# Attention and two feed-forward layers on one core: one more row group in seven products, a shared last query tile, wider idle matmuls

## The chip, the cores and the metric

The kernel runs on one core of a Trainium2 chip. The metric is the device time in microseconds (us) of one execution, inputs in device memory at its start and the output there at its end. TensorE (PE in the profile) multiplies; VectorE (DVE), ScalarE (ACT) and GpSimd (POOL) do the elementwise work; SyncE (SP) issues nearly all DMAs, in order.

## The reference, cut to what matters

```python
# attention: 4 batches, 8 heads, 576 positions, head size 64, 128 random features
def phi(x):
    h = einsum('bhsd,md->bhsm', x, omega) - sum(x * x) / 2
    return exp(h - max(h, -1)) / sqrt(128)
q_p, k_p = phi(q * scale), phi(k * scale)
kv, z = einsum('bhsm,bhsd->bhmd', k_p, v), sum(k_p, 2)
x = einsum('bhsm,bhmd->bhsd', q_p, kv) / (einsum('bhsm,bhm->bhs', q_p, z)[..., None] + 1e-6)
x = x.transpose(0, 2, 1, 3).reshape(2304, 512)
h = x @ moe_w_in;  x = (h - tanh(h)) @ moe_w_out              # layer 1, d_ff = 2048
h = x @ moe2_w_in; out = (h * sigmoid(1.702 * h)) @ moe2_w_out  # layer 2, d_ff = 2048
```

## The kernel before, in words

The program is one stream per engine, in the order in which the code issues it; there is no scheduler. It has three stages.

**Attention** (`period(k)`, k = 0 to 15, and two tails) takes two heads at a time: 16 pairs. The pairs are software-pipelined: in one period TensorE projects the queries of pair k (`att_a`, L133) and the keys of pair k+1 (`att_b`, L161, L164), transposes the normalised result of pair k-2 (`att_e`, L237), builds key times value of pair k (`att_c`, L188, L192) and the numerators with their denominators of pair k-1 (`att_d`, L210). A pair's 576 queries are four tiles of 128 and a fifth that holds the last 64. In `att_d` each tile and head is one fp32 matmul: the exponentials of 128 queries are the stationary operand, key times value with its extra column (65 columns) the moving one. So there are 10 a pair, in two PSUM tiles (tags y2 and y3): six for tiles 0 to 2, four for tiles 3 and 4. The fifth tile starts at query 448, so it computes 64 queries a second time (`s0 = min(st * 128, S - 128)`), and only `tq[:, 64:128]` of its transpose is used. Every fp32 matmul but a transpose shows as two records.

Then VectorE adds the epsilon, takes the reciprocal and multiplies (`att_d_norm`, L222 to L224), TensorE transposes into y2 and y3, ScalarE rounds the transposed tile to the upper part (`att_e_hi`, L251) and VectorE subtracts it to get the lower part (`att_e_lo`, L256). Both parts are stored to the DRAM tensor `xs`, one DMA each (two each in the first batch, whose first 512 positions stay in SBUF). `xh` and `xl` have one buffer, so the next pair's write waits for the store. L210 of the next pair writes y2 and y3 again, so it waits for L256. VectorE also subtracts the maximum (L147) that GpSimd reduced over partitions (L143), and with ScalarE unpacks layer 1's weights (L293 to L327) in two periods of three.

**Layer 1** makes x in blocks of 512 rows and is not touched.

**Layer 2** has three row blocks of 768, each seen as two halves of 384, and eight pairs of 256 hidden columns: 24 groups (`GROUPS`), the last eight (n = 16 to 23) on the third block, with pair 7 first (`LAST`). Each group's hidden part h is made by a seven-product scheme (`h_prod`, L868): P1 to P7, six matmuls each, one a slot; a group has seven slots (`SLOTS`), and `q = 7 * n + s` counts them. The group's y part is made one group later. There are two ways: `y_chunk` (L889), eight chunks of six matmuls in `hs` banks; or, for the groups with `yform(n)`, that is `YG <= n < YE` (17 to 22), seven products P1 to P7 of six matmuls (`y_prod`, L929) in two PSUM tiles `ya` and `yc` of two banks each, with operands formed on GpSimd (`forms`) and combined output weights `wos`. `y_chunk` at a block's first group copies into `yacc`, later ones add (L899); `y_add` (L938) always adds.

The input forms of the third block (`xprep_ticks(2, ...)`) are 14 ticks, popped one a slot from q = 101: each casts on ScalarE (L432) and subtracts on GpSimd (kt = 0) or VectorE (kt = 1, L433), and some make a difference on VectorE first (L582). Their loads are issued at group 14, slot 0. The combined output weights of a pair are three more ticks (`L2_STICKS`): sums on GpSimd (L440), then two splits (L432, L433), each stored to `wfs`; in the code before, pair 7 has none.

At the program's start two matmuls on zeros (`warm_up(pt("y0")[:, :320], 2)`, L601) run while the first inputs arrive.

Of the kernel before, what the change touches and what calls it, by code (L numbers as in the profile page):

```python
# [25 lines left out]
DV = D + 1  # L26
# [29 lines left out]
L2_TICKS = {(0, 1): "a", (0, 5): "b", (1, 1): "s", (1, 2): "c", (1, 3): "h", (1, 5): "d", (1, 6): "o", (2, 0): "e"}  # L56
L2_STICKS = {2: "f", 3: "g", 6: "i"}
SLOTS = ("P1", "P7", "P6", "P4", "P5", "P2", "P3")
XID = dict(P2=0, P1=1, P7=2, P6=3, P4=4, P5=5, P3=6)

YG, YE = 2 * NPAIR + 1, 3 * NPAIR - 1
YP = ("P3", "P1", "P2", "P6", "P7", "P5", "P4")
# [4 lines left out]
def body(ctx, tc, qT, kT, v, om, w1, w2, out):  # L67
# [58 lines left out]
    def att_a(i):  # L126
# [7 lines left out]
        return a  # L134

    def att_a_copy(i, tiles, j):
        if j == 0:
            pqs[i] = ap.tile([128, 2, S], F32, tag="pq", name="pq", bufs=2)
        pq, r = pqs[i], rest[i]
        nc.scalar.copy(out=pq[:, j, 0:512], in_=tiles[j])  # L140
        nc.scalar.copy(out=pq[:, j, 512:S], in_=r[j][:, :S - 512])  # L141
        mqs[i, j] = ap.tile([128, S], F32, tag="mq", name="mq", bufs=2)
        nc.gpsimd.partition_all_reduce(  # L143
            mqs[i, j], pq[:, j, :], channels=128, reduce_op=bass.bass_isa.ReduceOp.max)

    def att_sub(i, j):
        nc.vector.tensor_tensor(out=pqs[i][:, j, :], in0=pqs[i][:, j, :], in1=mqs.pop((i, j)), op=ALU.subtract)  # L147

    def att_exp(i, j):
        nc.scalar.activation(out=pqs[i][:, j, :], in_=pqs[i][:, j, :], func=AF.Exp)  # L150

# [49 lines left out]
    def att_d(i):  # L201
        pq, kvz = pqs.pop(i), kvzs.pop(i)
        tags = ("y0", "y1") if i == N16 - 1 else ("y2", "y3")
        for g, d, tag in (((0, 1, 2), pn1, tags[0]), ((3, 4), pn2, tags[1])):
            pn = pt(tag)
            for k, st in enumerate(g):
                s0 = min(st * 128, S - 128)
                for j in range(2):
                    c = (2 * k + j) * DV
                    nc.tensor.matmul(  # L210
                        pn[:, c:c + DV], pq[:, j, s0:s0 + 128], kvz[:, j * DV:j * DV + DV],
                        start=True, stop=True)
            d[i] = pn
        xts[i] = ap.tile([128, ST, 2, D], F32, tag="xt", name="xt", bufs=2)
# [25 lines left out]
    def att_e_parts(i, tiles):  # L240
        tp, tq = tiles
        b, p = divmod(i, NP)
        xh = ap.tile([128, S], F32R, tag="xh", name="xh", bufs=1)
        xl = ap.tile([128, S], F32R, tag="xl", name="xl", bufs=1)
        xd = xblk[0, 0]
        h0, l0 = (xd[:, 0, p, :], xd[:, 1, p, :]) if b == 0 else (xh[:, :512], xl[:, :512])
        return (h0, l0, tp), (xh[:, 512:], xl[:, 512:], tq[:, 64:128]), xh, xl

    def att_e_hi(parts):
        for h, l, src in parts[:2]:  # L250
            nc.scalar.copy(out=h, in_=src)  # L251

    def att_e_lo(i, parts):
        b, p = divmod(i, NP)
        for h, l, src in parts[:2]:
            nc.vector.tensor_tensor(out=l, in0=src, in1=h.bitcast(F32), op=ALU.subtract)  # L256
        c0 = 512 if b == 0 else 0
        for hl, t in ((0, parts[2]), (1, parts[3])):
            nc.sync.dma_start(out=xs[hl, p, :, b * S + c0:b * S + S], in_=t[:, c0:].bitcast(F32))
            if b == 0:  # L260
                nc.sync.dma_start(out=xs[hl, p, :, :512], in_=parts[0][hl].bitcast(F32))

# [202 lines left out]
    def conv_ticks(p, pairs, place=None):  # L465
# [208 lines left out]

    warm_up(pt("y0")[:, :320], 2)
    tiles, mx = att_b(0)
# [395 lines left out]
    for n in range(NG + 1):  # L1072
        sb, j = GROUPS[min(n, NG - 1)]
        for s in range(7):
# [50 lines left out]
            if xticks:  # L1125
                if 3 <= q < 98 and q != 6 or q > 100:
                    xticks.popleft()()
# [6 lines left out]
            if ticks and at >= 0:  # L1134
                for x in L2_TICKS.get((at // 7 % 2, s), "") + (L2_TICKS.get((2, s), "") if at >= 14 and at // 7 % 2 == 0 else ""):
                    if ticks[0][0] == x:
                        ticks.popleft()[1]()
            if sticks and at >= 14 and at // 7 % 2 == 0 and s in L2_STICKS:
                assert sticks[0][0] == L2_STICKS[s]
                sticks.popleft()[1]()  # L1140
            if n == 14 and s == 0:
                assert not ticks and not sticks
# [62 lines left out]
```

## Time and profile before

| | |
|---|---|
| time, median of 3 runs | 893.46 us (893.02 to 893.53) |
| the profiled execution | 894.37 us, its span 892.6 us |
| TensorE busy | 887.0 us, 99% of the span, 5154 matmul records |
| VectorE, ScalarE, GpSimd busy | 624.1, 575.5 and 528.3 us |
| HBM traffic | 171 GB/s over the span |

The span runs from the first to the last instruction; the 1.8 us beside it are what lies around it. A busy time is the union of an engine's records, and a record is longer than the step from one start to the next, since each is pipelined into the one before: lengths of steps are read from starts.

### The profile page before, as it was taken

What the parts mean: (1) busy time and instruction counts of PE and PEld (TensorE: products, weight loads), DVE (VectorE), ACT (ScalarE), POOL (GpSimd) and SP (SyncE); (2) the same over time, 40 slices, a digit from 0 to 9 for tenths busy, and PEclk for the clock granted to TensorE, in tenths of its full rate; (3) what the DMA queues carried; (4) which work ended last, traced back from release to release, by engine and by line L of the source; (5) the groups of instructions that cost most, each with busy time, mean ns of one, the idle gap of its engine ahead of it and who ended that gap; (6) DMA issues with size and microseconds to landing.
All of it is one profiled execution on the core that took longest, in us unless ns stands there. A gap on an engine that the chain in (4) does not pass through costs nothing.

```text
span 892.6 us, 14447 instructions
## 1 busy us (share of the span) xinstructions
PE 887.0 (99%) x5154; PEld 812.3 (91%) x5154; DVE 624.1 (70%) x956; ACT 575.5 (64%) x1205; POOL 528.3 (59%) x424
## 2 busy tenths in 40 slices
PE   9999999999999999999999999999999999999998
PEld 7999988888899888888898899999999999999997
DVE  5999978766666665787767457477877778445555
ACT  6999978787777766877667644446565554434442
POOL 3555535566656655777765556537657565347774
PEclk9999999999999999999999999999999999999999
DMA  7888855043353440695471560824553241376751
GB/s 237 249 265 258 280 172 176 24 142 104 109 189 117 143 142 24 186 325 197 166 270 48 207 217 3 289 97 179 201 203 145 90 131 48 112 301 235 296 224 71
DMA packets 55815, 153.38 MB, mean 172 GB/s; under 512 B 6336, under 2 KB 13120, under 8 KB 52672
## 3 DMA queue, kind: packets, MB, share of 16 engines
q1 hardware_dynamic: 55600, 152.15, 49.3%
q8 instruction: 40, 0.66, 0.3%
q10 hardware_dynamic: 144, 0.33, 0.1%
q14 instruction: 31, 0.25, 0.1%
HBM read 105.27 MB, written 47.19 MB: 171 GB/s over the span
## 4 chain that ended last, share of the span: by engine, by line
PE 97%; DVE 2%; POOL 1%; DMA 0%; issue 0%; ACT 0%; POOLq 0%
PE y L391 22%; PE hs L353 22%; PE y L868 19%; PE hs L889 17%; PE yb L929 5%; PE y L210 4%; PE y L192 2%; PE y L133 2%; PE hs L161 1%; PE hs L868 1%; PE y L237 1%; PE hs L164 1%; POOL mq L143 1%; DVE pq L147 0%; DMA kt<-kT 0%
## 5 line engine op out<-in xcount | busy, mean ns | idle before, releaser
L353 PE MATMUL hs<-xb,w 128*128 128x512 f32 (+1 forms) x960 | 209.2, 368 | 0.0
L353 PEld LDWEIGHTS hs<-xb,w 128*128 128x128 f32 x960 | 167.5, 189 | 30.0
L868 PE MATMUL y<-x,win 128*128 128x384 f32 x966 | 193.1, 334 | 0.0
L391 PE MATMUL y<-ghi,w 128*128 128x512 f32 (+1 forms) x640 | 192.4, 368 | 0.1
L367 POOL TENSOR_TENSOR glo<-wq,ghi 128x512 fp32r<-128x512 f32 x72 | 101.0, 1403 | 136.9 <-ACT ghi L365 135.3
L868 PEld LDWEIGHTS y<-x,win 128*128 128x128 f32 x966 | 169.7, 188 | 0.0
L889 PE MATMUL hs<-g,wout 128*128 128x384 f32 x864 | 169.1, 334 | 0.0
L383 DVE COPY_PREDICATED wq<-m,t 128x512 f32<-128x512 uint16 x72 | 88.6, 1230 | 104.8 <-POOL wq L381 103.7
L889 PEld LDWEIGHTS hs<-g,wout 128*128 128x128 f32 x864 | 151.4, 188 | 0.4 <-DVE yacc L938 0.3
L391 PEld LDWEIGHTS y<-ghi,w 128*128 128x128 f32 x640 | 116.6, 189 | 20.6 <-issue 0.5
L977 POOL TENSOR_TENSOR g<-sg,g 128x384 fp32r<-128x384 f32 x84 | 96.7, 1159 | 48.0 <-ACT g L976 24.9
L391 PE MATMUL y<-glo,w 128*128 128x512 f32 (+1 forms) x320 | 117.8, 368 | 0.0
L899 DVE TENSOR_TENSOR yacc<-hs,yacc 128x384 f32<-128x384 f32 x120 | 65.7, 552 | 51.4 <-PE hs L889 50.9
L381 POOL TENSOR_TENSOR wq<-wq,s 128x512 f32<-128x512 f32 x70 | 90.6, 1294 | 18.6 <-DVE wq L380 18.6
L143 POOL PARTITION_ALL_REDUCE mq<-pq x32 | 67.0, 2140 | 53.1 <-ACT pq L141 45.0
L373 ACT ACTIVATE s<-hs 128x512 f32<-128x512 f32 x72 | 43.0, 598 | 61.4 <-PE hs L353 61.3
L391 PEld LDWEIGHTS y<-glo,w 128*128 128x128 f32 x320 | 60.4, 189 | 9.9
L964 ACT ACTIVATE sg<-y 128x384 f32<-128x384 f32 x57 | 28.1, 494 | 62.9 <-DVE y L949 58.1
L304 DVE SCALAR_TENSOR_TENSOR raw<-raw 128x512 int32<-128x512 int32 x57 | 62.8, 1101 | 1.6
L938 DVE TENSOR_TENSOR yacc<-yb,yacc 128x768 f32<-128x768 f32 x42 | 40.2, 958 | 33.7 <-PE yb L929 33.5
L365 ACT CAST ghi<-wq 128x512 fp32r<-128x512 f32 x72 | 44.3, 616 | 27.8 <-DVE wq L383 27.7
L380 DVE SCALAR_TENSOR_TENSOR wq<-wq,hs 128x512 f32<-128x512 f32 x72 | 49.1, 681 | 13.3 <-ACT t L375 13.2
(146 smaller groups left out, 1470.5 us busy)
## 6 DMA issues: line engine op xcount, KB each, us to landing
raw<-w SPq DMA_DIRECT2D x57, 512.0 KB, 4.6
xb<-xs SPq DMA_DIRECT2D x24, 512.0 KB, 6.0
win<-wfi SPq DMA_DIRECT2D x9, 1280.0 KB, 6.7
wout<-wfo SPq DMA_DIRECT2D x9, 1024.0 KB, 7.4
wos<-wfs SPq DMA_DIRECT2D x6, 1024.0 KB, 8.8
vt<-v SPq DMA_DIRECT2D x16, 325.0 KB, 3.9
kt<-kT SPq DMA_DIRECT2D x15, 320.0 KB, 3.4
qt<-qT SPq DMA_DIRECT2D x16, 288.0 KB, 3.2
```

Source lines behind the costliest of these rows:

```text
L143: nc.gpsimd.partition_all_reduce(mqs[i, j], pq[:, j, :], channels=128, reduce_op=bass.bass_isa.ReduceOp.max)
L304: nc.vector.scalar_tensor_tensor(out=c, in0=c, scalar=3, in1=z, op0=ALU.logical_shift_left, op1=ALU.bitwise_or)
L353: nc.tensor.matmul(h[:, j * n:j * n + n], w[:, 0, a, kt * 128:kt * 128 + 128], x[:, c, kt, :n], start=(k == 0), stop=(k == 11))
L367: nc.gpsimd.tensor_tensor(out=lo, in0=g, in1=hi.bitcast(F32), op=ALU.subtract)
L380: nc.vector.scalar_tensor_tensor(out=w, in0=w, scalar=QC, in1=h, op0=ALU.add, op1=ALU.mult)
L381: (nc.vector if si < 2 else nc.gpsimd).tensor_tensor(out=w, in0=w, in1=s, op=ALU.mult)
L383: nc.vector.copy_predicated(out=w, mask=m.bitcast(mybir.dt.uint16), data=t)
L391: nc.tensor.matmul(y[d][:, :n], w[:, 1, a, d * 128:d * 128 + 128], g[c][:, j * n:j * n + n], start=(first and j == 0 and k == 0), stop=(la ...
L868: nc.tensor.matmul(dst, w[:, WID[name], a, kt * 128:kt * 128 + 128], xt[:, kt, c, :], start=(first and k == 0), stop=(k == 5), skip_group_ ...
L889: nc.tensor.matmul(dst, wout[j][:, f, a, d * 128:d * 128 + 128], gt[n, f, t][:, c, :], start=(k == 0), stop=(k == 5))
L899: nc.vector.tensor_tensor(out=u, in0=dst, in1=u, op=ALU.add)
L977: nc.gpsimd.tensor_tensor(out=u[:, 1, :], in0=g, in1=u[:, 0, :].bitcast(F32), op=ALU.subtract)
```

## The change

It does five things.

1. `YG` goes from 17 to 16: group 16, the third block's first, makes y from seven products. As it is the first of its block, four of its `y_add`s copy into a new `yacc` (those of P3, P1, P6 and P7, in which a quarter comes first). With n even, P1's tile gets tag `ya`; a tile of tag `yc` is opened ahead of it and not used, so that `yc` has the pool's first two banks and `ya` the other two.
2. Pair 7 gets its combined weights: `f`, `g` and `i` for all pairs, in group 14 at slots 2, 3 and 5.
3. The loads of the third block's input move from group 14, slot 0, to its slot 6, and the 14 ticks from q = 101 to 114, one a slot, to q = 107 to 114, one or two a slot (`X2_TICKS`).
4. In attention the last 64 queries of both heads stand side by side in `pq` (columns 512 to 639). One matmul takes these 128 as the stationary operand and both heads' key times value (130 columns) as the moving one; each head's answer is a block of 64 by 65 in it. It takes the place of two. The fifth tile's transpose, cast and subtraction cover 128 columns and not 64, and its stores are two a part, 64 partitions by 64 columns each.
5. The two first matmuls on zeros have 400 columns and not 320.

```diff
-YG, YE = 2 * NPAIR + 1, 3 * NPAIR - 1
+YG, YE = 2 * NPAIR, 3 * NPAIR - 1
+X2_TICKS = {2: 2, 3: 2, 4: 2, 5: 1, 6: 2, 7: 1, 8: 2, 9: 2}
...
-        nc.scalar.copy(out=pq[:, j, 0:512], in_=tiles[j])
-        nc.scalar.copy(out=pq[:, j, 512:S], in_=r[j][:, :S - 512])
+        nc.scalar.copy(out=pq[:, j * 640:j * 640 + 512], in_=tiles[j])
+        nc.scalar.copy(out=pq[:, 512 + j * 64:576 + j * 64], in_=r[j][:, :S - 512])
...
-                s0 = min(st * 128, S - 128)
+                if st == 4:
+                    nc.tensor.matmul(pn[:, 2 * k * DV:2 * (k + 1) * DV], pq[:, 512:640], kvz, start=True, stop=True)
+                    continue
...
-        return (h0, l0, tp), (xh[:, 512:], xl[:, 512:], tq[:, 64:128]), xh, xl
+        return (h0, l0, tp), (xh[:, 512:], xl[:, 512:], tq[:, :128])
...
-        for hl, t in ((0, parts[2]), (1, parts[3])):
-            nc.sync.dma_start(out=xs[hl, p, :, b * S + c0:b * S + S], in_=t[:, c0:].bitcast(F32))
-            if b == 0:
-                nc.sync.dma_start(out=xs[hl, p, :, :512], in_=parts[0][hl].bitcast(F32))
+        for hl in range(2):
+            main, last = parts[0][hl].bitcast(F32), parts[1][hl].bitcast(F32)
+            nc.sync.dma_start(out=xs[hl, p, :, b * S:b * S + 512], in_=main)
+            for j in range(2):
+                q = slice(64 * j, 64 * j + 64)
+                nc.sync.dma_start(out=xs[hl, p, q, b * S + 512:b * S + S], in_=last[q, q])
...
-        extra = [(x, f) for q in pairs if q < NPAIR - 1 for x, f in dict(
+        extra = [(x, f) for q in pairs for x, f in dict(
...
-    warm_up(pt("y0")[:, :320], 2)
+    warm_up(pt("y0")[:, :400], 2)
...
+        if n == YG and name in ("P1", "P6", "P7", "P3"):
+            u = yacc[sb, t, h] = ya_tile("yacc")
+            nc.vector.tensor_copy(out=u, in_=src)
+            return
...
+                psb.tile([128, 2, 512], F32, tag="yc", name="yb", bufs=1)
...
-                if 3 <= q < 98 and q != 6 or q > 100:
+                for _ in range((3 <= q < 98 and q != 6) + X2_TICKS.get(q - 105, 0)):
...
-            if sticks and at >= 14 and at // 7 % 2 == 0 and s in L2_STICKS:
-                assert sticks[0][0] == L2_STICKS[s]
-                sticks.popleft()[1]()
-            if n == 14 and s == 0:
+            if sticks and at >= 14 and at // 7 % 2 == 0:
+                x = L2_STICKS.get(s + (n == 14 and s > 4))
+                if x:
+                    assert sticks[0][0] == x
+                    sticks.popleft()[1]()
+            if n == 14 and s == 6:
```

TensorE in attention, one pair before, from the transpose of pair k-2 to the next pair's queries (`y` are the PSUM tiles, `pq` the exponentials, `kvz` key times value):

```order
L237 MATMUL y_450<-ident,xt 128x128
L188 MATMUL y_478<-vt,kp 128x130
L192 MATMUL y_478<-vt,kp 128x65 x8
L210 MATMUL y_496<-kvz,pq 128x65 x6
L210 MATMUL y_503<-kvz,pq 128x65 x4
L133 MATMUL y_521<-qt,omd 128x512
```

The same place in the changed program:

```order
L244 MATMUL y_450<-ident,xt 128x128
L192 MATMUL y_480<-vt,kp 128x130
L196 MATMUL y_480<-vt,kp 128x65 x8
L217 MATMUL y_498<-kvz,pq 128x65 x6
L217 MATMUL y_505<-kvz,pq 128x65 x2
L213 MATMUL y_505<-kvz,pq 128x130
L134 MATMUL y_522<-qt,omd 128x512
```

Ten numerator matmuls became nine, the last of them 130 columns wide; nothing else on TensorE moved there.

SP's queue in the same stage, one pair of a later batch before:

```order
L113 DMA qt<-qT 128x576
L118 DMA kt<-kT 128x640
L259 DMA xs<-xh 128x576
L259 DMA xs<-xl 128x576
L123 DMA vt<-v 128x650
L281 DMA raw<-w 128x1024
```

And in the changed program:

```order
L114 DMA qt<-qT 128x576
L119 DMA kt<-kT 128x640
L266 DMA xs<-xh 128x512
L269 DMA xs<-xh 64x64 x2
L266 DMA xs<-xl 128x512
L269 DMA xs<-xl 64x64 x2
L124 DMA vt<-v 128x650
L289 DMA raw<-w 128x1024
```

Two stores a pair became six, all ahead of the loads of `vt` and `raw`.

TensorE in layer 2, end of group 16's hidden part and its y part before (`g` are the activated hidden parts; the h products of group 17 stand between):

```order
L868 MATMUL y_8317<-x_7856,win 128x384 x6
L889 MATMUL hs<-g_8211,wout 128x384 x3
L889 MATMUL hs<-g_8278,wout 128x384 x3
L868 MATMUL y_8292<-x_7873,win 128x384 x6
L889 MATMUL hs<-g_8211,wout 128x384 x3
L889 MATMUL hs<-g_8278,wout 128x384 x3
L868 MATMUL y_8317<-x_7903,win 128x384 x6
L889 MATMUL hs<-g_8211,wout 128x384 x3
L889 MATMUL hs<-g_8278,wout 128x384 x3
L889 MATMUL hs<-g_8211,wout 128x384 x3
L889 MATMUL hs<-g_8278,wout 128x384 x3
```

The same place after:

```order
L876 MATMUL y_8369<-x_7887,win 128x384 x6
L937 MATMUL yb<-g_8264,wout 128x384 x6
L876 MATMUL y_8345<-x_7909,win 128x384 x6
L937 MATMUL yb<-g_8331,wout 128x384 x6
L876 MATMUL y_8369<-x_7938,win 128x384 x6
L937 MATMUL yb<-fT_8382,wos 128x384 x6
L876 MATMUL y_8345<-x_7958,win 128x384 x6
L937 MATMUL yb<-fT_8409,wos 128x384 x6
```

The slot with two chunks is gone: each slot now holds one h product and one y product.

## Rows read from the trace of the kernel before

**Rows 1.** Page, busy time of each engine
```profile
PE 887.0 (99%) x5154; PEld 812.3 (91%) x5154; DVE 624.1 (70%) x956; ACT 575.5 (64%) x1205; POOL 528.3 (59%) x424
```
**Rows 2.** Stretches of one pair, sum of three: length, engines, clock, DMA share, GB/s
```profile
41.90:49.23 7.33, 7.33 (x72) 6.67 (x71) 6.96 (x16) 6.79 (x21) 4.03 (x2) 1.00 0.94 289
...
sum 21.99, PE 21.99 PEld 20.01 DVE 20.92 ACT 20.41 POOL 12.80; mean PE 7.33 PEld 6.67 DVE 6.97 ACT 6.80 POOL 4.27
```
**Rows 3.** TensorE in order of time, one pair: start, us, instruction, records
```profile
45.24 0.39 PE L188 MATMUL y<-vt,kp 128*128 128x130 f32 x2
45.46 1.90 PE L192 MATMUL y<-vt,kp 128*128 128x65 f32 x16
47.20 2.40 PE L210 MATMUL y<-kvz,pq 128*128 128x65 f32 x20
49.52 0.69 PE L133 MATMUL y<-qt,omd 64*128 64x512 f32 x1
```
**Rows 4.** VectorE in order of time, two pairs, with idle time ahead
```profile
41.41 0.17 DVE L222 TENSOR_SCALAR rc<-y 128x6 f32<-128x6 f32 x1 [0.34 <-PE y L210]
...
45.95 0.69 DVE L256 TENSOR_TENSOR xb<-y,xb 128x512 fp32r<-128x512 f32 x1
46.56 0.21 DVE L256 TENSOR_TENSOR xl<-y,xh 128x64 fp32r<-128x64 f32 x1
...
48.74 0.16 DVE L222 TENSOR_SCALAR rc<-y 128x6 f32<-128x6 f32 x1 [0.17 <-PE y L210]
```
**Rows 5.** ScalarE in order of time, the casts of one pair
```profile
45.33 0.59 ACT L251 CAST xb<-y 128x512 fp32r<-128x512 f32 x1
45.81 0.22 ACT L251 CAST xh<-y 128x64 fp32r<-128x64 f32 x1
```
**Rows 6.** Line 259, the stores: SP's issue ns min/median/max, starts, and landing
```profile
L259 SPq DMA_DIRECT2D xs<-xl x16: 320/327/558, 25.1 to 132.9; - x16
...
DMA to landing us min/median/max: 1.7/2.8/5.1
```
**Rows 7.** DMA issues, first batch: KB each, median us to landing
```profile
xs<-xb SPq DMA_DIRECT2D x8, 256.0 KB, 2.9
...
xs<-xh SPq DMA_DIRECT2D x4, 32.0 KB, 2.2
xs<-xl SPq DMA_DIRECT2D x4, 32.0 KB, 2.7
```
**Rows 8.** TensorE in order of time, the program's start
```profile
1.50 2.50 PE L601 MATMUL y<-warm 128*128 128x320 f32 x4 [1.50 <-DVE warm L100]
4.23 0.76 PE L157 MATMUL hs<-omd,kt 128*128 128x128 f32 x2 [0.23 <-DMA kt<-kT]
4.92 2.08 PE L161 MATMUL y<-omd,kt 64*128 64x128 f32 x16
...
8.82 1.23 PE L161 MATMUL hs<-omd,kt 64*128 64x128 f32 x16
```
**Rows 9.** TensorE in order of time, two slots of group 16
```profile
766.72 1.20 PE L889 MATMUL hs<-g,wout 128*128 128x384 f32 x6
...
768.80 2.24 PE L889 MATMUL hs<-g,wout 128*128 128x384 f32 x12
```
**Rows 10.** Stretches of groups 14 and 15, columns as in Rows 2
```profile
730.32:745.92 15.60, 15.60 (x92) 15.60 (x92) 10.75 (x18) 7.70 (x17) 8.37 (x8) 1.00 0.18 51
745.92:761.52 15.60, 15.60 (x92) 15.60 (x92) 13.89 (x20) 7.73 (x19) 8.04 (x8) 1.00 0.22 75
```
**Rows 11.** VectorE in order of time, input forms of block 3
```profile
756.54 0.54 DVE L433 TENSOR_TENSOR x<-xi,x 128x384 fp32r<-128x384 f32 x1
757.01 1.37 DVE L582 TENSOR_TENSOR xi<-xi 128x384 f32<-128x384 f32 x1
```
**Rows 12.** Line 440, ns min/median/max: the dearest of four sums
```profile
L440 POOL TENSOR_TENSOR ssum<-raw x4: 1303/1303/1312, 611.8 to 705.8; 128x256 f32<-128x256 f32 x4
```
**Rows 13.** Loads of the input forms: KB each, median us to landing
```profile
xi<-ysf SPq DMA_DIRECT2D x12, 384.0 KB, 5.5
```

More of the change, by code (lines that the diff above doesn't have):

```diff
@@ L137, in att_a_copy @@
         if j == 0:
-            pqs[i] = ap.tile([128, 2, S], F32, tag="pq", name="pq", bufs=2)
+            pqs[i] = ap.tile([128, 2 * S], F32, tag="pq", name="pq", bufs=2)
         pq, r = pqs[i], rest[i]
-        nc.scalar.copy(out=pq[:, j, 0:512], in_=tiles[j])
-        nc.scalar.copy(out=pq[:, j, 512:S], in_=r[j][:, :S - 512])
+        nc.scalar.copy(out=pq[:, j * 640:j * 640 + 512], in_=tiles[j])
+        nc.scalar.copy(out=pq[:, 512 + j * 64:576 + j * 64], in_=r[j][:, :S - 512])
         mqs[i, j] = ap.tile([128, S], F32, tag="mq", name="mq", bufs=2)
         nc.gpsimd.partition_all_reduce(
-            mqs[i, j], pq[:, j, :], channels=128, reduce_op=bass.bass_isa.ReduceOp.max)
+            mqs[i, j], pq[:, j * S:j * S + S], channels=128, reduce_op=bass.bass_isa.ReduceOp.max)
     def att_sub(i, j):
-        nc.vector.tensor_tensor(out=pqs[i][:, j, :], in0=pqs[i][:, j, :], in1=mqs.pop((i, j)), op=ALU.subtract)
+        pq = pqs[i][:, j * S:j * S + S]
+        nc.vector.tensor_tensor(out=pq, in0=pq, in1=mqs.pop((i, j)), op=ALU.subtract)
     def att_exp(i, j):
-        nc.scalar.activation(out=pqs[i][:, j, :], in_=pqs[i][:, j, :], func=AF.Exp)
+        pq = pqs[i][:, j * S:j * S + S]
+        nc.scalar.activation(out=pq, in_=pq, func=AF.Exp)
     def att_b(i):
@@ L210, in att_d @@
                     nc.tensor.matmul(
-                        pn[:, c:c + DV], pq[:, j, s0:s0 + 128], kvz[:, j * DV:j * DV + DV],
-                        start=True, stop=True)
+                        pn[:, c:c + DV], pq[:, j * 640 + st * 128:j * 640 + st * 128 + 128],
+                        kvz[:, j * DV:j * DV + DV], start=True, stop=True)
             d[i] = pn
@@ L242, in att_e_parts @@
         b, p = divmod(i, NP)
-        xh = ap.tile([128, S], F32R, tag="xh", name="xh", bufs=1)
-        xl = ap.tile([128, S], F32R, tag="xl", name="xl", bufs=1)
+        xh = ap.tile([128, 640], F32R, tag="xh", name="xh", bufs=1)
+        xl = ap.tile([128, 640], F32R, tag="xl", name="xl", bufs=1)
         xd = xblk[0, 0]
         h0, l0 = (xd[:, 0, p, :], xd[:, 1, p, :]) if b == 0 else (xh[:, :512], xl[:, :512])
-        return (h0, l0, tp), (xh[:, 512:], xl[:, 512:], tq[:, 64:128]), xh, xl
+        return (h0, l0, tp), (xh[:, 512:], xl[:, 512:], tq[:, :128])
     def att_e_hi(parts):
-        for h, l, src in parts[:2]:
+        for h, l, src in parts:
             nc.scalar.copy(out=h, in_=src)
@@ L254, in att_e_lo @@
         b, p = divmod(i, NP)
-        for h, l, src in parts[:2]:
+        for h, l, src in parts:
             nc.vector.tensor_tensor(out=l, in0=src, in1=h.bitcast(F32), op=ALU.subtract)
-        c0 = 512 if b == 0 else 0
-        for hl, t in ((0, parts[2]), (1, parts[3])):
-            nc.sync.dma_start(out=xs[hl, p, :, b * S + c0:b * S + S], in_=t[:, c0:].bitcast(F32))
-            if b == 0:
-                nc.sync.dma_start(out=xs[hl, p, :, :512], in_=parts[0][hl].bitcast(F32))
+        for hl in range(2):
[4 more added lines that the diff above has]
+                nc.sync.dma_start(out=xs[hl, p, q, b * S + 512:b * S + S], in_=last[q, q])
     wt = {}
@@ L1152, in body @@
                 xticks.extend(xt)
-                new_x2(2, 0)
             if n == 14:
+                if s == 0:
+                    new_x2(2, 0)
                 if SLOTS[s] != "P2":
```

## The prediction

> **What bounds the kernel now.** I read the busy times first. TensorE is busy for 887.0 of 892.6 us [rows 1], so a microsecond taken out of its queue is worth one, unless an engine that feeds it becomes the bound in that stage. So I then read the two stages that the change touches by stretches. In attention a pair takes 7.33 us; three pairs are 21.99 us, in which TensorE is busy throughout, VectorE 20.92 and ScalarE 20.41 [rows 2]. The reader is to see how little is left: VectorE has 1.07 us in three pairs. In layer 2, groups 14 and 15 take 15.60 us each, TensorE busy throughout; VectorE goes from 10.75 to 13.89 us, and GpSimd, at 8.37 and 8.04, is half empty [rows 10]. Last I read single instructions in order of time, taking steps from one start to the next. At 0.2% (1.8 us) a measurement of this kernel can't tell a gain from none.
>
> **Attention's numerators.** TensorE: the twenty records of ten 65-column matmuls take 2.32 us by starts (47.20 to 49.52), 0.116 each; sixteen records of the same width take 1.74 (45.46 to 47.20), 0.109 each; the two records of one 130-column matmul take 0.22 (45.24 to 45.46), 0.11 each [rows 3]. A record of 130 columns thus steps like one of 65 here, and what goes is one matmul of two, 0.22 to 0.23 us a pair, for 16 pairs 3.6 us.
>
> [...]
>
> VectorE pays for it. Its subtraction for the fifth tile covers 128 columns: 512 take 0.69 us and 64 take 0.21 [rows 4], so 1.07 ns a column, +0.07 us a pair. On ScalarE it is (0.59 - 0.22)/448 = 0.83 ns a column [rows 5], +0.05 us, and it has 1.58 us to spare in three pairs. VectorE would be at 20.92 + 0.21 = 21.13 us in three pairs, while TensorE falls to 21.99 - 0.67 = 21.32. That almost meets. TensorE's L210 waits for VectorE's L256 of the pair before, since they share a PSUM tile. Bounds: at the cheap end VectorE's order fits and the whole 3.6 us stays. At the other, only its idle time that the rows print, 0.34 us in one pair and 0.17 in the next, mean 0.25 [rows 4], can close, and the 0.07 of new work comes off: 0.18 a pair, 2.9 us; were only the smaller wait usable, it is 0.17 - 0.07 = 0.10, 1.6 us. If nothing can close, the pairs lengthen by the 0.07, +1.1 us. I take 3.0 (0.19 a pair), between the first two ends and nearer the pair's mean: printed lengths overlap (45.95 + 0.69 ends after 46.56, where the next starts [rows 4]), so true idle time is a little longer than what is printed. From the tails and the first pair nothing is subtracted separately; they lie within 3.6 to 1.6.
>
> **Attention's stores.** Each pair had two or four stores and has six. SP issues one in 0.33 us and they land after 1.7 to 5.1, median 2.8 [rows 6]; four more put the last issue 1.3 us later. The first of a pair starts near VectorE's end of L256, 46.8, so the last is issued near 48.5. The next pair's ScalarE cast comes one period after 45.33, and VectorE's part, whose buffer the last stores empty, after 45.95 [rows 4, 5]: 45.95 + 7.1 = 53.1. There are 4.6 us for a landing whose median is 2.8, so the cost is 0; a landing of 5.1 each time would be 0.5 late.
>
> The first batch already issues 32 KB stores of 64 columns a row, and they land in 2.2 and 2.7 us, where the 256 KB ones take 2.9 [rows 7]. [...]
>
> **Group 16's y part.** Eight chunks of six matmuls become seven products of six. A slot with twelve takes 2.24 us, one with six 1.20 [rows 9], 1.04 less on TensorE, and no other engine is near its bound: -1.04. What hides the rest: GpSimd forms operands in group 17's slots, as it does for the groups after; VectorE's four copies and three adds replace eight copies.
>
> **Pair 7's weights and the input forms.** GpSimd gets four sums, the dearest 1.30 us [rows 12], so at most 5.2 us, and two splits, which I price like the sums at 2.6. Even all of this in group 14 would make 8.37 + 7.8 = 16.2 of 15.60 [rows 10]; three x subtractions move out of that group to the next, about as long, which leaves near 12. VectorE's part is tighter: the input forms, spread over groups 14 and 15 before, now all lie in 15 and one slot of 16, two a slot. Its input work is 13.89 us there already, and some three operations of 0.54 (alone) to 1.37 us (what one takes beside GpSimd [rows 11]) come in: +1.6 to +4.1, so 15.5 to 18.0 in a group of 15.60. The excess runs over into group 16, which has room behind; TensorE only waits if a form comes after its product. P2's is needed first, at q = 110, three slots after the first tick, two of which take two ticks each; later ones fall due one slot after another. Bounds: 0 (order holds) to 2.4 (all of 18.0 - 15.6). I take 0.1, at the low end, since products ask for forms at about the rate at which ticks make them. The loads are issued three slots ahead of their first use, as before; 5.5 us to landing [rows 13] against three slots of 1.04 + 1.04 [rows 9], 6.2 us.
>
> **The matmuls on zeros.** Two of 320 columns start at 1.50 and show 2.50 us, to 4.00; the first real matmul waits 0.23 us more for its input until 4.23 [rows 8]. With 25% more columns they would show up to 0.62 more, to 4.62. A group's printed end is 0.16 past the step (six records show 1.20 [rows 9] and six more add 1.04), and part of the 2.50 does not grow with columns, so the first matmul comes between 0 and 0.4 late; I take +0.1.
>
> What this does to the clock is open. [...]
>
> **The sum.** -3.0 - 1.04 + 0.1 + 0.1 = -3.84 on a span of 892.6: 888.76. With the 1.8 us around it, 890.5 against the profiled 894.37. That execution is 0.9 above the median of 893.46, so the comparable median is 893.46 - 3.84 = 889.6; as the overlap of VectorE's records may give a little more, I say **889.5**.
>
> **The rivals.**
> [...]
> - Forms come late in group 15 (the VectorE sum of 15.5 to 18.0 decides, above some 17): about 2 us, 891.5. For it: 13.89 us busy before. Against: work ahead of its due time, and group 16's room.
> - The other side: the stores come late. If a pair's last store lands after more than the 4.6 us above, the next pair's L256 waits, L210 behind it, and VectorE has nothing to make up for it. Priced at 0.5 us beyond (5.1, the longest landing seen [rows 6]) in the twelve pairs of the later batches: 12 x 0.5 = 6, so 895.5. It decides from a landing of about 4.6; the median is 2.8, though DMA is busy for 0.94 of a pair's time [rows 2].
> - The wide matmul costs two narrow ones: 3.0 less gained, 892.5. The 0.11 us at both widths [rows 3] speaks against it.
>
> **How the numbers follow.** Forecast 0.50, earlier clock 0.24, late forms 0.12, late stores 0.06, columns 0.03, something else 0.05. The forecast's own range is 888.2 to 891.0 (attention 3.6 to 1.6 and the other small ends in part). The whole range, 887.3 to 892.1, takes in the earlier clock with its 2.4 against the smaller gains, and late forms; late stores and the columns' rule fall out, with half of the rest. Faster by over 0.2% means under 891.7: the forecast, the clock and most of the late forms, less a little, 0.83; within 0.2%: columns, some late forms and rest, 0.09; slower: late stores and rest, 0.08.
>
> **What would show it.** In attention a pair's period should fall from 7.33 to about 7.14 us, L210's eighteen records (0.11 each) with no idle time ahead of TensorE larger than 0.05; if VectorE binds, its idle time is 0 and TensorE shows waits for L256. Group 16 to 17 should lose 1.04 us. Group 15's VectorE row should read about 15 us with TensorE still at 15.60 of its stretch. [...] Stores landing beyond 4.6 us with VectorE waiting for `xh` or `xl` would make the prediction wrong, as would a 130-column record of L213 stepping by 0.22.

## The result, and the profile after

The changed kernel is slower.

| | before | after |
|---|---|---|
| time, median of 6 runs each | 893.5 us (892.85 to 893.98) | 900.84 us (899.06 to 906.06) |
| after / before | | 1.0089, 95% interval 1.0075 to 1.0103 |
| the profiled execution, its span | 894.37, 892.6 us | 900.0, 898.0 us |

The executions of the changed kernel differ by 7 us, and their spans go with the granted clock of TensorE: 896.9 us at 0.996, 898.0 and 898.2 at 0.994, 899.5 and 900.8 at 0.992, 904.1 at 0.987. In every execution of the kernel before that ran beside the experiments below it read 0.999 or 1.0. That is the first thing to see. One execution of all those below, 912.55 us in the eighth experiment, counts as slow (over 1.5% above the fastest of its kernel), so it is in that experiment's median and not in its ratio.

TensorE's busy time, against [rows 1], from the page of the kernel after:

```profile
PE 888.3 (99%) x5116; PEld 809.8 (90%) x5116; DVE 622.8 (69%) x955; ACT 579.6 (65%) x1210; POOL 539.1 (60%) x437
```

It has 38 records fewer and is busy 1.3 us longer: something runs slower. What TensorE waits for (engine, tile and line, the one waited for, total us, times, longest):

```profile
PE y L217 <- DVE xl L263: 2.1, 3, 0.8
...
PE y L217 <- DVE xb L263: 0.9, 2, 0.6
PE y L399 <- ACT ghi L373: 0.8, 1, 0.8
PE y L399 <- POOL glo L375: 0.7, 1, 0.7
```

L217 holds the numerators, L263 is VectorE's subtraction. Against the 7.33 us of every pair in [rows 2], three pairs after (length, then busy time of TensorE, its weight loads, VectorE, ScalarE and GpSimd, clock, DMA share, GB/s):

```profile
48.46:55.69 7.23, 7.23 (x68) 6.52 (x68) 7.15 (x15) 6.73 (x21) 4.24 (x2) 1.00 0.69 211
55.69:64.01 8.32, 7.68 (x68) 6.72 (x67) 7.35 (x16) 7.39 (x21) 4.03 (x2) 0.96 0.68 195
64.01:72.49 8.48, 8.48 (x69) 7.21 (x68) 6.28 (x16) 6.71 (x21) 3.91 (x2) 0.84 0.94 301
```

The first pair gains 0.10, as such pairs should; the second loses 0.99 and the third 1.15, though TensorE has no idle time in the third at all. TensorE in order of time across them (against [rows 3]):

```profile
55.69 0.69 PE L134 MATMUL y<-qt,omd 64*128 64x512 f32 x1
...
58.96 1.90 PE L196 MATMUL y<-vt,kp 128*128 128x65 f32 x16
61.50 2.04 PE L217 MATMUL y<-kvz,pq 128*128 128x65 f32 x16 [0.64 <-DVE xl L263]
63.33 0.75 PE L213 MATMUL y<-kvz,pq 128*128 128x130 f32 x2
64.01 1.22 PE L134 MATMUL y<-qt,omd 64*128 64x512 f32 x1
```

Ahead of L217 there is an idle gap of 0.64 us. From some 1.7 us after its end the records are longer: L213 shows 0.75 us, where it shows 0.44 in other pairs, and the same 512-column matmul 1.22 instead of 0.69. The stretches ahead of the gap's end, behind it, and from there on, with the clock in the third column from the right:

```profile
55.69:61.50 5.81, 5.17 (x51) 4.44 (x50) 5.69 (x12) 5.19 (x15) 3.86 (x2) 1.00 0.58 144
61.50:63.22 1.72, 1.72 (x15) 1.72 (x16) 0.94 (x3) 1.72 (x6) 0.17 (x1) 1.00 0.86 270
63.22:66.52 3.30, 3.30 (x15) 2.05 (x16) 2.81 (x8) 1.65 (x4) 0.00 (x0) 0.52 1.05 355
```

For 3.30 us TensorE is at its lower level, clock 0.52 in that stretch. By starts, the way from L217 at 61.50 to the second L134 behind it (72.49) takes 10.99 us; from the L217 at 39.09, behind a gap of the same length, it takes 9.37. So 1.62 us are lost, about half of the 3.30, for a gap of 0.64. The same, 10.99 us of way, follows the gap of 0.81 that ends at 78.46 and the one of 0.64 that ends at 109.64; the gap of 0.64 that ends at 39.09 is not followed by it.

**Why VectorE is late.** VectorE of the same pair, and GpSimd's all-reduces of it:

```profile
57.15 0.75 DVE L150 TENSOR_TENSOR pq<-pq,mq 128x576 f32<-128x576 f32 x1
57.82 1.63 DVE L335 TENSOR_TENSOR w<-raw,w 128x512 fp32r<-128x512 f32 x1
59.37 1.47 DVE L180 TENSOR_REDUCE mx<-hs 128x4 f32<-128x512 f32 x3
60.77 0.87 DVE L263 TENSOR_TENSOR xl<-y,xh 128x512 fp32r<-128x512 f32 x2
```

```profile
57.64 4.03 POOL L145 PARTITION_ALL_REDUCE mq<-pq  x2 [2.44 <-ACT pq L143]
```

The corresponding pair before:

```profile
58.72 0.69 DVE L327 TENSOR_TENSOR w<-raw,w 128x512 fp32r<-128x512 f32 x1
59.32 1.48 DVE L176 TENSOR_REDUCE mx<-hs 128x4 f32<-128x512 f32 x3
60.72 0.81 DVE L256 TENSOR_TENSOR xl<-y,xh 128x512 fp32r<-128x512 f32 x2
61.45 1.52 DVE L147 TENSOR_TENSOR pq<-pq,mq 128x576 f32<-128x576 f32 x1
```

```profile
58.80 4.37 POOL L143 PARTITION_ALL_REDUCE mq<-pq  x2 [2.70 <-DVE pq L147]
```

Before, VectorE's last operation ahead of the maxima starts 0.08 us ahead of the all-reduce and takes 0.69; the all-reduce is what takes longer (4.37 against 4.03). After, the all-reduce starts 0.18 us ahead, and the operation takes 1.63 instead of 0.69: VectorE has lost a race. The 0.94 us go straight to L263, which stands behind it. In attention after, four operations of 1.63 us stand ahead of L263 (L335 at 35.41, 57.82 and 105.96, L307 at 74.78); each is followed, 3.68 us after its start, by the end of one of the four gaps of 0.64 to 0.81. Before, from 20 us on, every operation of VectorE over 1 us in attention stands behind L256 (L304 and the L147 after it), where it delays nothing that TensorE waits for; the L147 of 1.52 us above is one. (In both orders above, what starts second takes longer. By how much hangs on more than the length of the first: in the ninth experiment an operation of VectorE that starts 0.07 us behind an all-reduce of 1.98 us takes 1.64 instead of 0.68 and ends 0.27 us before it, so it gets 0.96 us longer, about half the all-reduce. Why the two get in each other's way no run shows.)

**The start and layer 2.** Against [rows 8], the start after:

```profile
4.33 0.64 PE L161 MATMUL hs<-omd,kt 128*128 128x128 f32 x2
4.89 1.34 PE L165 MATMUL y<-omd,kt 64*128 64x128 f32 x16
```

The sixteen 128-column records from 4.89 take 1.34 us, where those from 4.92 in [rows 8] take 2.08. By the lengths of the records, the upper level is there from about 5.3 us instead of 9.1 (the profile's clock column prints 1.00 all through both starts), and the second pair's queries start at 10.94 instead of 12.78, 1.83 earlier. In layer 2 the slot with twelve matmuls of group 16's y part is gone, 1.04 us. Ahead of it, at the end of group 15, an h product starts 0.16 late and takes 0.13 longer than its like: its weight load waits for VectorE's L961, which stands among the input forms. So 0.75 is left.

The balance of this execution to the first matmul of layer 1 (121.47 before, 126.40 after): -1.83 at the start, -2.55 for fifteen pairs at 7.16, +3.39 for seven waits, +4.86 for three stretches at the lower level, and 1.06 over. Of that, some 0.8 are the five waits of L217 beyond their printed length: from L196's start to L217's it is 1.73 us without a gap, 2.53 or 2.54 with one of 0.64 and 2.70 with one of 0.81, 0.16 or 0.17 more than the printed gap. Layer 1 adds 1.6, most of it the two waits at L399 above (the seventh experiment finds their cause); layer 2 takes back 0.75, and what follows VectorE's last operation another 0.4.

### The profile page after: what moved, and what is told of

Same layout as the page of the kernel before. It is cut to its first block, busy times and chain, and to the rows that moved or that the text cites. A ratio compares the mean times of both kernels' runs of the same rounds, so it can differ in the third digit from the quotient of the medians.

```text
span 898.0 us, 14510 instructions
## 1 busy us (share of the span) xinstructions
PE 888.3 (99%) x5116; PEld 809.8 (90%) x5116; DVE 622.8 (69%) x955; ACT 579.6 (65%) x1210; POOL 539.1 (60%) x437
## 4 chain that ended last, share of the span: by engine, by line
PE 88%; DVE 6%; POOL 2%; ACT 2%; issue 1%; DMA 1%; SPq 0%; POOLq 0%; ACTq 0%; DVEq 0%
PE y L399 21%; PE hs L361 20%; PE y L876 19%; PE hs L897 16%; PE yb L937 6%; PE y L217 2%; PE y L134 1%; DVE pq L150 1%; POOL wq L389 1%; PE hs L876 1%; DVE w L335 1%; PE hs L165 1%; DVE mx L180 1%; PE y L196 1%; DMA xs<-xh 1%
## 5 line engine op out<-in xcount | busy, mean ns | idle before, releaser
L399 PE MATMUL y<-ghi,w 128*128 128x512 f32 (+1 forms) x640 | 192.5, 368 | 0.8 <-ACT ghi L373 0.8
L897 PE MATMUL hs<-g,wout 128*128 128x384 f32 x816 | 159.8, 334 | 0.0
L897 PEld LDWEIGHTS hs<-g,wout 128*128 128x128 f32 x816 | 143.0, 188 | 0.4 <-DVE yacc L950 0.3
L399 PEld LDWEIGHTS y<-ghi,w 128*128 128x128 f32 x640 | 116.6, 189 | 21.5 <-ACT ghi L373 1.2
L399 PE MATMUL y<-glo,w 128*128 128x512 f32 (+1 forms) x320 | 118.0, 369 | 0.7 <-POOL glo L375 0.7
L989 POOL TENSOR_TENSOR g<-sg,g 128x384 fp32r<-128x384 f32 x82 | 94.9, 1165 | 33.3 <-ACT g L988 22.9
L145 POOL PARTITION_ALL_REDUCE mq<-pq x32 | 64.8, 2074 | 60.6 <-ACT pq L143 60.6
L399 PEld LDWEIGHTS y<-glo,w 128*128 128x128 f32 x320 | 60.4, 189 | 10.9 <-POOL glo L375 1.1
L950 DVE TENSOR_TENSOR yacc<-yb,yacc 128x768 f32<-128x768 f32 x45 | 43.1, 957 | 36.7 <-PE yb L937 36.5
L312 DVE SCALAR_TENSOR_TENSOR raw<-raw 128x512 int32<-128x512 int32 x57 | 60.9, 1068 | 1.7
```

Source lines behind the costliest of these rows:

```text
L145: nc.gpsimd.partition_all_reduce(mqs[i, j], pq[:, j * S:j * S + S], channels=128, reduce_op=bass.bass_isa.ReduceOp.max)
L312: nc.vector.scalar_tensor_tensor(out=c, in0=c, scalar=3, in1=z, op0=ALU.logical_shift_left, op1=ALU.bitwise_or)
L399: nc.tensor.matmul(y[d][:, :n], w[:, 1, a, d * 128:d * 128 + 128], g[c][:, j * n:j * n + n], start=(first and j == 0 and k == 0), stop=(la ...
L897: nc.tensor.matmul(dst, wout[j][:, f, a, d * 128:d * 128 + 128], gt[n, f, t][:, c, :], start=(k == 0), stop=(k == 5))
L989: nc.gpsimd.tensor_tensor(out=u[:, 1, :], in0=g, in1=u[:, 0, :].bitcast(F32), op=ALU.subtract)
```

## The experiments

**1. Is it attention?** Attention as before (`pq`, the numerators, the fifth tile and the stores), with the rest of the change:

```diff
-                if st == 4:
-                    nc.tensor.matmul(pn[:, 2 * k * DV:2 * (k + 1) * DV], pq[:, 512:640], kvz, start=True, stop=True)
-                    continue
+                s0 = min(st * 128, S - 128)
...
```

> The changed kernel with attention as it was before; the group's seven products, the input forms' new place and the 400-column matmuls on zeros stay. The trace of the changed kernel puts -1.83 us on the start (the clock rises earlier) and -0.75 on groups 15 and 16 (-1.04 and a wait of 0.29). Theory G (attention's shorter TensorE part meets VectorE, TensorE idles ahead of the numerators, and the clock falls after some of these gaps): 893.5 - 1.8 - 0.75 = 890.9, no wait ahead of L210 and no stretch at the lower level after the start. Theory S (the six stores a pair come late and hold the engines up): also 890.9. Theory P (the earlier rise of the clock shifts attention against its loads and GpSimd, whatever the numerators do): waits ahead of L210 stay and it is above 895.

Measured: 891.62 us against 893.49, ratio 0.998 (0.9972 to 0.9989), clock 0.999 or more throughout. No wait ahead of the numerators is left:

```profile
PE y L602 <- DVE warm L101: 1.5, 1, 1.5
PE hs L162 <- ACT kp L182: 0.2, 1, 0.2
```

Theory P falls. This version beats both kernels.

**2. Attention alone**, on the kernel before (the same functions, the other way round).

> The kernel before with attention's part of the change alone (320-column matmuls on zeros, group 16 as before). Theories G and S: the loss is all in here, +6.8 us by the first matmul of layer 1 and +1.7 in its first hundred us, so about 902, with runs spread by several us. Theory P: with the start as before, attention gains as forecast, about 890.5.

Measured: 900.54 us (897.44 to 903.69), ratio 1.0076 (1.0054 to 1.0099). The loss is in attention's part. (7.05 us lost here and 1.87 gained in the first experiment don't add up to the whole change's 7.3: the executions with attention's part differ by 6 to 7 us.) In this trace the clock rose at 7.6 us with 320 columns, and at 9.1 in the kernel before with the same start: its rise moves by itself.

**3. TensorE's part of a pair as long as before, the rest as changed:**

```diff
                     nc.tensor.matmul(pn[:, 2 * k * DV:2 * (k + 1) * DV], pq[:, 512:640], kvz, start=True, stop=True)
+                    nc.tensor.matmul(pn[:, 4 * DV:5 * DV], warm[:, :128], warm[:, :DV], start=True, stop=True)
```

> The changed kernel with one matmul on zeros, 65 columns (0.22 us, two records), behind the wide numerator matmul of each pair, into unused columns of its tile: TensorE's part of a pair is 7.33 us again, while VectorE's 128-column subtraction and the six stores stay. Theory G: VectorE (about 7.04 us a pair) has room again, the waits ahead of L217 go, the clock stays up, and it is 890.9 to 891.5. Theory S: the stores are as late as they were, the waits stay, and it is 899 or more, as the pairs lengthen besides.

Measured: 893.66 us, ratio 0.9998 (0.999 to 1.0007): 0.22 us of useless work a pair makes the kernel 7.2 us faster. Two pairs of it:

```profile
48.62:55.95 7.33, 7.33 (x70) 6.67 (x69) 7.21 (x16) 6.69 (x21) 4.40 (x2) 1.00 0.82 263
55.95:63.28 7.33, 7.33 (x70) 6.67 (x69) 6.74 (x15) 6.96 (x21) 4.37 (x2) 1.00 0.75 234
```

The stores and VectorE's wider tile are still in it, so they don't make the waits ahead of the numerators. In its trace no single operation of VectorE ahead of L263 takes over 1 us: no race is lost. It is 2 us above the first experiment and 2.2 above the upper end of what I expected; by the starts, 1.2 of that come in layer 1, where one wait of 0.7 for ScalarE (L400) stands.

**4. The shortening alone**, on the kernel before, with its casts, subtraction and stores:

```diff
                 s0 = min(st * 128, S - 128)
+                if st == 4:
+                    nc.tensor.matmul(pn[:, 2 * k * DV:2 * (k + 1) * DV], pq[:, 0, s0:s0 + 128], kvz, start=True, stop=True)
+                    continue
```

> The kernel before with nine numerator matmuls instead of ten, the last 130 columns wide, and nothing else changed: casts, subtraction and stores as before. It leaves out the second head's last 64 queries (computed from the first head's). Theory G, if the shortening alone does it: TensorE's 7.11 us a pair meets VectorE's 6.97 plus its waits, gaps of 0.2 to 0.8 us ahead of L210, the clock falls: 896 to 902. Theory G, if VectorE's added 0.07 us a pair tips it, and theory S (the stores): the pairs take 7.11 and it is 890.

Measured: 899.49 us, ratio 1.006 (1.004 to 1.008). Nothing was added to any other engine, and 0.2 us less work a pair for TensorE makes it 6 us slower. One gap with the race that it follows, and the clock behind it:

```profile
101.16 4.00 POOL L143 PARTITION_ALL_REDUCE mq<-pq  x2 [3.65 <-ACT pq L141]
101.31 1.63 DVE L302 SCALAR_TENSOR_TENSOR raw<-raw 128x512 int32<-128x512 int32 x1
```

```profile
104.99 2.11 PE L213 MATMUL y<-kvz,pq 128*128 128x65 f32 x16 [0.81 <-DVE xl L259]
106.89 0.75 PE L209 MATMUL y<-kvz,pq 128*128 128x130 f32 x2
107.57 1.22 PE L133 MATMUL y<-qt,omd 64*128 64x512 f32 x1
```

```profile
104.99:106.71 1.72, 1.72 (x15) 1.72 (x16) 1.48 (x4) 1.46 (x6) 0.17 (x1) 1.00 0.54 188
106.71:110.08 3.37, 3.37 (x16) 2.11 (x16) 2.81 (x8) 1.35 (x3) 0.00 (x0) 0.50 0.94 271
```

Four operations of 1.63 or 1.64 us stand ahead of L259 in this trace, each starts 3.68 us before the end of one of four gaps of 0.64 to 0.81, and the second experiment's trace shows the same four times. So the shorter numerators by themselves lose the races.

Its executions part the loss: the one with clock 1.0 spans 893.5 us, those with 0.996 some 896, those with 0.992 899 to 899.6; the kernel before spans 891.7 in the median. So by that one execution the waits outweigh the shorter pairs by 1.8 us, and the clock adds up to 6.

**5. and 6. Can order repair it?** In one, L263 goes ahead of the maxima:

```diff
+        if k > 1:
+            att_e_lo(k - 2, parts)
         if k + 1 < N16:
             for t in range(3):
                 att_b_max(tiles, mx, t)
...
-        if k > 1:
-            att_e_lo(k - 2, parts)
```

> The changed kernel with VectorE's subtraction of the lower part (L263) issued ahead of the three maxima of the next keys (L180), not behind them. In the changed kernel's bad pairs a two-input operation of VectorE (L335 or L307, 0.68 us by itself) starts just after GpSimd's all-reduce instead of just before it and takes 1.63, and L263 stands behind that and behind 1.4 us of maxima. Theory R (the lost race makes L263 late, nothing else): with L263 1.4 us earlier the waits ahead of L217 go, all pairs take 7.16, the clock stays up: 891.6 (attention as before) less 15 x 0.17 plus the 1.2 us that the first layer lost in the run with the filling matmul, about 890. Theory B (VectorE's work with its collisions simply doesn't fit 7.16 us, wherever L263 stands): VectorE stays the bound, waits appear at other places, 895 or more.

Measured: 911.69 us, ratio 1.0188 (1.0171 to 1.0205). TensorE's waits moved:

```profile
PE y L134 <- ACT kvz L202: 11.9, 14, 1.1
```

The maxima came later, ScalarE's exponentials of the keys with them, and the copy of key times value (L202) behind those; L134 needs the tile that it empties. L263's place was not free to give. In the other, the two weight operations go behind L263:

```diff
-        for x in last:
-            conv4(US[x], nc.vector)
-        for x in old:
-            conv2a(US[x])
...
             att_e_lo(k - 2, parts)
+        for x in last:
+            conv4(US[x], nc.vector)
+        for x in old:
+            conv2a(US[x])
```

> The changed kernel with the two weight operations of VectorE that lose the race (L335 and L307) issued behind L263 instead of ahead of the next keys' maxima. Theory R: L263 stands behind nothing that waits for GpSimd; no waits ahead of L217, about 890. Theory B: the same operations now meet the second all-reduce of the pair or push the subtraction of the maximum (L150) back; TensorE waits there for the exponentials and it is 895 or more.

Measured: 902.08 us, ratio 1.0093 (1.0079 to 1.0107), with the waits back at L217:

```profile
PE y L217 <- DVE xl L263: 2.8, 4, 0.8
...
PE y L217 <- DVE xb L263: 1.1, 2, 0.8
```

For these two orders theory R is wrong as I put it, that only L263's place matters. In the last trace no operation of VectorE ahead of L263 takes over 1 us, so no race is lost there; in the pairs with gaps of 0.84 us VectorE stands idle for 0.20 ahead of L263, waiting for ScalarE's cast (L258). What else makes L263 late there I did not settle. Neither order holds 7.16 us.

**7. The stores.** The third experiment's kernel with the two stores a part as before:

```diff
-            nc.sync.dma_start(out=xs[hl, p, :, b * S:b * S + 512], in_=main)
-            for j in range(2):
-                q = slice(64 * j, 64 * j + 64)
-                nc.sync.dma_start(out=xs[hl, p, q, b * S + 512:b * S + S], in_=last[q, q])
+            nc.sync.dma_start(out=xs[hl, p, :, b * S + c0:b * S + S], in_=t[:, c0:S].bitcast(F32))
...
```

> The changed kernel with the 65-column matmul on zeros (893.66 us) and two stores a part and pair as before instead of six in all; the last 64 queries of the second head land wrongly. The first layer took 1.2 us longer there than with attention as before, with one wait of 0.7 us for ScalarE at 180. If the four added stores cause this: 892.4. If VectorE's and ScalarE's wider tile does: 893.7.

Measured: 892.18 us, ratio 0.9982 (0.9973 to 0.9991), 1.5 below the third experiment; no wait in layer 1 is left. The four added stores cost some 1.5 us. Where, the traces show: in attention's last pair, whose cast ScalarE does after layer 1 has begun. With six stores (third experiment) and with two (here):

```profile
130.88 0.75 ACT L259 CAST xh<-y 128x512 fp32r<-128x512 f32 x2 [2.52 <-DMA xs<-xh]
```

```profile
129.59 0.75 ACT L259 CAST xh<-y 128x512 fp32r<-128x512 f32 x2 [1.29 <-PE y L245]
```

With two stores this cast starts 5.5 us after the one before it, not a period of 7.3, and `xh` has one buffer: with six stores it waits until those of the pair before have landed. ScalarE's and GpSimd's work for layer 1 stands behind it and is still 1.17 us late at 179.65, where TensorE waits. The same wait, of 2.1 to 3.4 us, stands in the traces of the changed kernel and of the second, third, fifth, sixth and ninth experiments, and in none with two stores; layer 1, from its first matmul to layer 2's, takes 394.1 to 395.1 us in those six, and 392.7 to 393.0 in the seven with two stores.

**8. Does a gap by itself bring the clock down?** The kernel before, VectorE held up in four pairs:

```diff
-            nc.vector.tensor_tensor(out=l, in0=src, in1=h.bitcast(F32), op=ALU.subtract)
+            for _ in range({2: 2, 5: 3, 8: 4, 11: 3}.get(i, 1) if src is parts[0][2] else 1):
+                nc.vector.tensor_tensor(out=l, in0=src, in1=h.bitcast(F32), op=ALU.subtract)
```

> The kernel before, with the 512-column subtraction (L256) of pairs 2, 5, 8 and 11 done 2, 3, 4 and 3 times: VectorE is 0.6, 1.2, 1.8 and 1.2 us late in four pairs, so that TensorE idles about 0.2, 0.8, 1.4 and 0.8 us there, and nothing else is changed. Theory G (a gap of this size can bring the clock down): stretches at the lower level of about 3.3 us after two to four of the gaps, 1.65 us each; 893.5 + 4 (the gaps with 0.2 each for the restart) + 3 to 7 = 901 to 904, and executions that differ by multiples of 1.65. If the clock falls for another reason than the gap: 897.5, granted clock 1.0.

Measured: 909.65 us in the median, ratio 1.0136 (1.0096 to 1.0175), with executions at 898.7 to 898.8 and at 907.5 to 912.6. The profiled one, 898.74, has the gaps and no stretch at the lower level:

```profile
62.86 2.42 PE L210 MATMUL y<-kvz,pq 128*128 128x65 f32 x20 [0.97 <-DVE xl L257]
...
86.73 2.42 PE L210 MATMUL y<-kvz,pq 128*128 128x65 f32 x20 [1.70 <-DVE xl L257]
```

Two executions, this one among them, span 896.6 us at clock 0.999; four span 905.3 to 907.8 at 0.989 to 0.991. Same program, same gaps: with gaps the clock can come down, and whether it does differs by execution; without them, in the kernel before, it read 0.999 or 1.0 every time. It cost more than I expected, 8.7 to 11.2 us of span; how those executions look inside no trace shows.

**9. and 10. GpSimd's share.** One all-reduce a pair instead of two:

```diff
+        if j:
+            mqs[i, 1] = mqs[i, 0]
+            return
         mqs[i, j] = ap.tile([128, S], F32, tag="mq", name="mq", bufs=2)
```

> The changed kernel with one all-reduce a pair on GpSimd instead of two (2.04 us less of 4.0); the second head subtracts the first head's maximum, so its answers differ in rounding at best. VectorE's work is the same, 7.05 us a pair. Theory C (GpSimd's all-reduce keeps VectorE's two-input operations on SBUF waiting, about a us a time, and that makes L263 late): half of the collisions go, no waits of 0.6 us ahead of L217, pairs of 7.16, the clock stays up: 891.6 - 2.6 + 1.5 (what the stores cost in layer 1) = 890.5. Theory V (VectorE's own work doesn't fit 7.16): the waits stay, 897 to 901.

Measured: 900.28 us (895.22 to 903.35), ratio 1.007 (1.0044 to 1.0095); the profiled execution is one of 896.51. By the time theory C loses. By the trace two races are still lost, each with its gap, 3.68 us after the operation's start as above. VectorE, GpSimd and TensorE at the second:

```profile
53.57 1.64 DVE L310 SCALAR_TENSOR_TENSOR raw<-raw 128x512 int32<-128x512 int32 x1
```

```profile
53.50 1.98 POOL L148 PARTITION_ALL_REDUCE mq<-pq  x1 [5.18 <-ACT pq L143]
```

```profile
57.25 0.99 PE L220 MATMUL y<-kvz,pq 128*128 128x65 f32 x7 [0.81 <-DVE xl L266]
```

GpSimd was 0.07 us ahead. The first gap, of 0.81 us, ends at 31.54; the lower level behind it lasts 6.80 us (32.80 to 39.60, clock 0.50), twice the 3.30 above, and the second gap is not followed by it. From 66.6 us on, no race is lost for six pairs, TensorE waits for nothing, and each takes 7.16 to 7.24:

```profile
66.62:73.78 7.16, 7.16 (x69) 6.45 (x68) 6.40 (x16) 6.92 (x21) 2.18 (x1) 1.00 0.83 277
73.78:81.00 7.22, 7.22 (x68) 6.51 (x67) 6.90 (x17) 7.13 (x22) 2.53 (x1) 1.00 0.72 236
81.00:88.16 7.16, 7.16 (x68) 6.44 (x67) 5.80 (x15) 6.48 (x20) 2.18 (x1) 1.00 0.85 277
```

VectorE's own work fits, so theory V is out; and its busy time there, 19.10 us in three pairs with one all-reduce each against the 20.92 of [rows 2] with two, shows that those held time lost beside GpSimd as well. What theory C says of single operations stands in the trace (the 1.64 us of L310, whose median in the changed kernel, as L307, is 0.68), its size in the times does not: one all-reduce is enough to lose races and the clock.

L335 on GpSimd:

```diff
         for x in last:
-            conv4(US[x], nc.vector)
+            conv4(US[x], nc.gpsimd)
```

> The changed kernel with the weights' subtraction of the attention stage (L335, 0.68 us of VectorE) on GpSimd (1.31 us there) in two pairs of three. Theory V: VectorE falls to some 6.6 us a pair, the waits go, 890.5. Theory C: GpSimd is active for 5.3 us of such a pair and VectorE has 2.6 us of two-input operations on SBUF left; together 7.9 of 7.16, so the waits ahead of L217 stay or grow: 900 or more.

Measured: 996.65 us, ratio 1.1158 (1.1142 to 1.1174). It tells nothing between V and C: L335 waits for ScalarE in GpSimd's queue, the all-reduces stand behind it, and TensorE waits for what follows from them:

```profile
PE y L244 <- DVE rc L229: 47.5, 8, 9.0
```

**11. and 12. The other parts.** The kernel before with 400 columns only:

```diff
-    warm_up(pt("y0")[:, :320], 2)
+    warm_up(pt("y0")[:, :400], 2)
```

> The kernel before with 400-column matmuls on zeros at the start and nothing else. In the traces the clock rose at 9.1 us (before), at 7.6 in three runs with 320 columns and at 5.3, 5.5, 6.2 and 6.2 with 400. If the wider matmuls bring it forward by some 1.5 to 2 us on average, half of it is gained: 893.6 - 1.1 = 892.5. If the rise only falls by chance: 893.6.

Measured: 893.43 us against 893.77, ratio 0.9997 (0.9989 to 1.0006): not told from none, though the level changes at about 6.1 us in its trace. And the layer 2 part only (`YG`, `X2_TICKS`, `extra`, the stick slots, `y_add`):

```diff
-YG, YE = 2 * NPAIR + 1, 3 * NPAIR - 1
+YG, YE = 2 * NPAIR, 3 * NPAIR - 1
...
```

> The kernel before with group 16's seven products, pair 7's weights and the input forms' new place alone. From the trace of the changed kernel: -1.04 on group 16 and a wait of 0.29 for a form ahead of it: 893.6 - 0.75 = 892.85. If the matmuls that replace the chunks cost more than the chunks saved elsewhere (VectorE's adds, the loads): 893.6 or more.

Measured: 892.37 us, ratio 0.9988 (0.998 to 0.9997): 1.1 us gained by the ratio (0.3 to 1.8 by its interval), near the 1.04 of the removed slot.

## Why the prediction was wrong

The step that failed is the one on attention's numerators, -3.0 us: measured, the part alone is +7.05 (900.54 against 893.49). Its bounds, -3.6 to +1.1, did not hold it, since they contain neither the waits in single pairs nor the clock.

- *A 130-column record steps like one of 65.* Right: undisturbed pairs fell from 7.33 to 7.16 us, and no run shows the columns' rule that the whole range leaves out.
- *VectorE has 1.07 us of idle time in three pairs; the sum is 21.13 of 21.32.* This is where it failed. I added means of busy time. But the busy time held up to 0.8 us by which single operations take longer beside GpSimd (L147 at 61.45 took 1.52 us, and takes 0.75 where it meets nothing), as the ninth experiment shows in sum, and which operations those are hangs on orders that are decided by 0.08 us (58.72 against 58.80). With TensorE 0.17 us a pair shorter, the all-reduce came first in four pairs, the longer operation (1.63 us) stood ahead of L263 instead of behind it, and no mean shows that. The 1.22, 1.46 and 1.52 us of VectorE's operations beside GpSimd could be read in the trace before; I looked at such a pair in layer 2 [rows 11] and not here.
- *That a stall costs its length*, as my bounds take without saying so. Wrong: gaps of 0.64 and 0.81 us took 1.62 us more by the clock, in three cases of four, and the eighth experiment shows the same program with and without that loss. I weighed the clock only at the start [rows 8].
- *The stores cost 0.* Off by some 1.5 us. The late stores of the rivals were there, once and not in twelve pairs: I gave every cast a period after the one before, but attention's last comes 5.5 us after, and it waited for the stores.
- *VectorE's 0.07 us of new work a pair.* Not what decides: the fourth experiment does without it and loses 6 us.
- *Group 16, -1.04.* Right in mechanism, and in size as far as 1.1 with its interval tells. *Forms, +0.1:* at most 0.29 in the changed kernel's trace, none in that of the twelfth experiment.
- *The matmuls on zeros, +0.1 and an open clock.* The first matmul came 0.10 late (4.33 against 4.23). No run shows the 2.4 us that the whole range takes in for an earlier clock: in this trace the rise came at 5.3 us and 1.83 us were gained; but over traces it came between 7.6 and 10.4 with 320 columns (five traces) and between 5.2 and 7.6 with 400 (nine). So it seems to come earlier with 400, yet the times of the eleventh experiment show no gain that can be told from none; that stays open.

No rival held what made the time: the earlier clock showed in this trace and the late stores once, and the chance of slower stood at 0.08, because no rival let TensorE itself get slower from getting less work.

## What to carry to other kernels

Where an engine is busy for the whole of a tightly pipelined stage, ask of each of its feeders which order of two engines' operations lets it be on time, and by how much; an order that holds by 0.08 us is not slack, and a busy time that is longer beside another engine (1.63 us against 0.69 here) is not all work of its own. A short idle gap of TensorE can cost more than twice its length through the clock (1.62 us here for one of 0.64, and nothing for another of 0.64), so redundant work that keeps it running is not free to remove: test a shortening by putting the same time back as work on zeros. Split a change by parts before it is taken as one: here one part lost 7.05 us and the others together gained 1.87. And look at the ends of a pipelined stage too: where its last steps follow each other faster than a period (5.5 us against 7.3 here), a buffer that was free in time all along may not be.

## What the runs showed of the hardware that I had not expected

- In a stage where TensorE is otherwise never idle, one gap of 0.64 us was followed, 1.7 us after its end, by 3.30 us at the lower level (clock 0.52 in that stretch). The gap of the same length that ended 22 us earlier was not, and one of 0.81 us in the ninth experiment was followed by 6.80 us.
- Four gaps of 0.34 to 1.70 us left the clock up in two executions of one program; four others of it, at clock 0.989 to 0.991, span 8.7 to 11.2 us more.
- An operation of VectorE that starts 0.07 to 0.18 us behind GpSimd's all-reduce takes 1.63 or 1.64 us instead of 0.69, and all of it counts as busy time; two all-reduces of which the first starts 0.08 us behind VectorE take 4.37 us instead of 4.03.
